# An unused strip of 96 bytes at the top of SBUF, in a kernel with two MLP layers behind a spectral layer

## The chip, the cores and the metric

The kernel runs on one core of a Trainium2 chip. The metric is the device time of one execution in microseconds (us); the times before are given as the median of three runs. All arithmetic is in float32, or in the float32 form that TensorE takes in one pass (fp32r), with each operand split into a high and a low part where one pass would lose too much.

## What is computed

The reference chains three parts over 2 x 3008 tokens of width 256:

```python
X = np.fft.rfft(x, axis=1)                      # along the 3008 positions
Yr = Xr @ w_r - Xi @ w_i + b_r
Yi = Xr @ w_i + Xi @ w_r + b_i
Yr, Yi = soft_threshold(Yr, 0.01), soft_threshold(Yi, 0.01)
x = np.fft.irfft(Yr + 1j * Yi, n=3008, axis=1).reshape(6016, 256)

h = x @ w_in            # 256 -> 2048
x = (h * sigmoid(1.702 * h)) @ w_out            # 2048 -> 256
h = x @ w_in2
out = (h * sigmoid(h)) @ w_out2
```

## The kernel before

The two Fourier transforms are matmuls with folded cosine and sine matrices (line 341 forward, line 344 back), the frequency-wise product with w_r and w_i is line 469, and the thresholds are lines 486 and 487. The result lies in one big tile, yt, of 128 partitions x 2 x 6016 floats; both MLP layers read it and write back into it in place.

The MLP takes its tokens in blocks of 1024 (five of them, and one of 896), each cut into two halves of 512 (448) columns. `group(l, i, p, hook)` handles layer l, block i and one pair p of hidden chunks of 128: there are 2 x 6 x 8 = 96 such pairs. In each it makes seven products of the input weights (line 736, by a Strassen-like scheme), each of three matmuls (high by high, high by low, low by high): 21 matmuls. The activation is line 739, its high part line 741, its low part line 746. The products with the output weights are `out_mm` (line 708): 24 matmuls for each pair. So a pair is 45 matmuls, and each has a moving operand of 512 or 448 columns and its own weight load of 128 x 128.

The moving operands of line 736 are tiles named x, those of line 708 tiles named g. Both, and the tiles of the earlier stages that have the same life (xt, f, fl, fd), are slots of 2048 bytes of the pool "xt": 14 slots of class x0 and 12 of class x1. The pool is opened on the right side of SBUF, whose pools are laid from the top of the memory downwards in the order in which they are opened: "xt" first, then, in turns, "lv0", "wc", "mid" and "yt". What is opened later on that side lies below. The pools of the left side (m, the weights, cv, raw and others) are laid from the bottom upwards and are not touched by what happens on the right side. The stationary operands of the MLP, wi and wo, are on the left side; those of the inverse transform are fh on the left and fl in slots of "xt", with slices of m (left side) as moving operands.

The scheduler places instructions with a timing of its own where the code does not fix their order; nearly all of the MLP is under a fixed order (`region('rest0')` and the like).

Of the kernel before, what the change touches and what calls it, by code (L numbers as in the profile page):

```python
# [9 lines left out]
F32 = mybir.dt.float32  # L10
# [11 lines left out]
P = 128  # L22
# [34 lines left out]
def spectral_mlp_kernel(ctx, tc, xin, mfwd, minv, wc, bias, w_in1, w_out1, w_in2, w_out2, outT):  # L57
# [11 lines left out]
    def region(name):  # L69
        m = CFG.get(name, "none")  # L70
        if "man" in ex:
            ex.pop("man").close()
        ex["man"] = ExitStack()
        if m != "none":
            ex["man"].enter_context(tc.manual_schedule(engines=None if m == "all" else {getattr(mybir.EngineType, e) for e in m.split(",")}))


    def opened(name, side=None, bufs=1, **kw):
        ex[name] = ExitStack()
        return ex[name].enter_context(tc.tile_pool(name=name, bufs=bufs, side=side, reuse_waits="tile", **kw))  # L80

    def closed(*names):
        for name in names:
            ex.pop(name).close()
# [2 lines left out]
    wia_p = opened("wia", "left", NPR // 2)  # L87
    cv_p = opened("cv", "left", 2)
    dram_p = opened("dram", bufs=1, space=bass.MemoryType.DRAM)
    xt_p = opened("xt", "right", 12)  # L90
    ps_p = [opened(f"ps{i}", bufs=4, space=PS) for i in range(2)]

# [235 lines left out]
    xt = {}  # L328
# [220 lines left out]
    yt = yt_p.tile([P, 2, NT], F32, name="yt")  # L549
# [330 lines left out]
    while pend:  # L880
        out_next()
    region('end')
    closed("ps1", "ps0", "wib", "yt", "xt", "cv", "wia", "m", "dram")

# [143 lines left out]
```

## Time and profile before

| | |
|---|---|
| median of three runs | 1226.17 us (1226.07 to 1228.11) |
| the profiled execution | 1227.75 us, span of its instructions 1225.6 us |
| mean granted TensorE clock | 0.998 |
| TensorE busy | 1193.8 us (97%) |
| ScalarE busy | 751.5 us (61%) |
| VectorE busy | 670.7 us (55%) |
| GpSimd busy | 526.9 us (43%) |

TensorE's row counts a matmul from its start to a modelled end, and matmuls overlap, so the duration of one is longer than its share of the time. The distance between two starts is what one costs; the chain of work that ended last and the listing in order of time show starts. Weight loads (PEld) run beside matmuls.

### The profile page before, as it was taken

The page shows a single profiled execution, that of the slowest core. Times are in us where ns is not written, and L with a number is a line of the kernel's source. Part 1 is how long each engine was busy: PE and PEld are TensorE (multiplying, and loading weights), DVE is VectorE, ACT ScalarE, POOL GpSimd, SP SyncE. Part 2 cuts the span into 40 slices and gives each one's busy share as a digit, 9 for nine tenths or more (in the row PEclk, how much of TensorE's full clock was granted, in tenths as well). Part 3 has the DMA queues.
Part 4 walks back from the last instruction along what each step waited for, and adds up shares of the span by engine and source line. Part 5 has one row for each costly group of instructions (what it writes and reads, how often), then busy time and mean ns, then how long its engine had stood idle before and what let it go on. Part 6 is the DMA issues. An engine that isn't in the chain of part 4 may idle for free.

```text
span 1225.6 us, 14433 instructions
## 1 busy us (share of the span) xinstructions
PE 1193.8 (97%) x5044; PEld 934.9 (76%) x5044; DVE 670.7 (55%) x1001; ACT 751.5 (61%) x1422; POOL 526.9 (43%) x429
## 2 busy tenths in 40 slices
PE   7999988799999999999999999999999999999998
PEld 4744488577787887877888978878888888888897
DVE  6868999777447556366464463352442533523422
ACT  1433443577667667667667776675665766755665
POOL 2543334463444444444445755433333333333332
PEclk9999999999999999999999999999999999999999
DMA  7642121121011110110120100000000000000000
GB/s 255 195 150 87 43 101 60 28 67 35 26 44 35 40 38 26 52 43 26 35 60 9 53 26 26 1 35 1 1 35 1 1 35 1 35 1 1 35 1 30
DMA packets 27274, 54.44 MB, mean 44 GB/s; under 512 B 2369, under 2 KB 11585, under 8 KB 26434
## 3 DMA queue, kind: packets, MB, share of 16 engines
q1 hardware_dynamic: 26018, 45.03, 11.1%
q0 software_dynamic: 1184, 8.50, 1.9%
q8 instruction: 39, 0.64, 0.2%
q14 instruction: 33, 0.27, 0.1%
HBM read 41.85 MB, written 11.67 MB: 44 GB/s over the span
## 4 chain that ended last, share of the span: by engine, by line
PE 68%; DVE 15%; ACT 7%; issue 4%; DMA 4%; POOL 1%; SPq 0%; DVEq 0%; ACTq 0%; POOLq 0%
PE o L708 35%; PE x L736 32%; ACT yt L739 2%; ACT g L741 2%; DMA raw<-in_wo 1%; DMA raw<-in_wi 1%; PE psf L341 1%; DVE fl L99 1%; DVE yt L628 1%; DVE f L501 1%; DVE cv_a L169 1%; DVE cv_c L167 1%; DVE th L487 1%; DMA raw<-in_x 1%; DVE cv_c L168 1%
## 5 line engine op out<-in xcount | busy, mean ns | idle before, releaser
L746 POOL TENSOR_TENSOR g<-yt,g 128x512 fp32r<-128x512 f32 (+1 forms) x282 | 368.1, 1318 | 533.3 <-DVE g L746 278.6
L708 PE MATMUL o<-g,wo 128*128 128x512 f32 (+1 forms) x2304 | 574.2, 391 | 4.6 <-POOL wo L99 4.6
L736 PE MATMUL x<-x,wi 128*128 128x512 f32 (+1 forms) x2016 | 513.3, 393 | 10.5 <-DVE yt L757 4.2
L708 PEld LDWEIGHTS o<-g,wo 128*128 128x128 f32 x2304 | 432.1, 188 | 100.8 <-POOL wo L99 6.3
L736 PEld LDWEIGHTS x<-x,wi 128*128 128x128 f32 x2016 | 376.7, 188 | 103.3 <-DVE yt L778 5.3
L739 ACT ACTIVATE yt<-yt 128x512 f32<-128x512 f32 (+1 forms) x288 | 179.1, 622 | 283.0 <-DVE yt L778 232.7
L741 ACT CAST g<-yt 128x512 fp32r<-128x512 f32 (+1 forms) x384 | 234.1, 611 | 11.8
L778 DVE TENSOR_TENSOR yt<-yt,x 128x512 f32<-128x512 f32 (+1 forms) x96 | 64.8, 675 | 230.3 <-PE x L736 230.2
L757 DVE TENSOR_TENSOR yt<-yt,x 128x512 f32<-128x512 f32 (+1 forms) x96 | 64.9, 676 | 163.5 <-ACT yt L755 159.3
L746 DVE TENSOR_TENSOR g<-yt,g 128x512 fp32r<-128x512 f32 (+1 forms) x102 | 71.1, 697 | 75.0 <-ACT g L741 73.8
L469 PE MATMUL psm<-wc_s,xt 128*128 128x512 f32 x192 | 84.5, 592 | 0.0
L469 PEld LDWEIGHTS psm<-wc_s,xt 128*128 128x128 f32 x192 | 36.4, 190 | 43.4 <-issue 41.2
L341 PE MATMUL psf<-m,xf 128*128 128x376 f32 (+2 forms) x208 | 61.4, 458 | 7.3 <-DVE xf L300 6.2
L659 DVE TENSOR_TENSOR x<-yt,x 128x512 fp32r<-128x512 f32 (+1 forms) x48 | 46.5, 970 | 34.6 <-ACT x L656 34.6
L781 DVE TENSOR_TENSOR yt<-yt,x 128x512 f32<-128x512 f32 (+1 forms) x96 | 64.8, 675 | 0.6
L341 PEld LDWEIGHTS psf<-m,xf 128*128 128x128 f32 x208 | 39.4, 200 | 28.7 <-DVE xf L300 7.3
L739 ACT ACTIVATE yt<-x 128x512 f32<-128x512 f32 (+1 forms) x96 | 56.2, 585 | 2.2 <-PE x L736 2.2
L772 ACT COPY yt<-x 128x512 f32<-128x512 f32 (+1 forms) x96 | 55.7, 581 | 0.8 <-PE x L736 0.8
L755 ACT COPY yt<-x 128x512 f32<-128x512 f32 (+1 forms) x96 | 54.9, 571 | 2.1 <-PE x L736 2.1
L770 ACT COPY yt<-x 128x512 f32<-128x512 f32 (+1 forms) x96 | 54.9, 572 | 0.0
L344 PE MATMUL psi<-m,fh 128*128 128x376 f32 (+3 forms) x208 | 48.0, 319 | 3.6 <-DVE rt L607 2.8
L224 POOL TENSOR_TENSOR cv_a<-cv_a,cv_c 128x512 f32<-128x512 f32 x26 | 37.9, 1457 | 14.6 <-DVE cv_c L171 10.6
(90 smaller groups left out, 798.3 us busy)
## 6 DMA issues: line engine op xcount, KB each, us to landing
raw<-in_wi SPq DMA_DIRECT2D x32, 256.0 KB, 3.1
raw<-in_wo SPq DMA_DIRECT2D x16, 512.0 KB, 3.6
raw<-in_x SPq DMA_DIRECT2D x12, 512.0 KB, 5.1
out_t<-yt SPq DMA_DIRECT2D x20, 256.0 KB, 2.0
m<-in_mi POOLq DMA_DIRECT2D x4, 1128.0 KB, 6.0
w_out<-cv_a SPq DMA_DIRECT2D x13, 256.0 KB, 2.0
cv_ld<-w_out SPq DMA_DIRECT2D x13, 256.0 KB, 2.6
m<-in_mi POOLq DMA_DIRECT2D x2, 1134.0 KB, 6.0
```

Of the source, the lines that this page charges most:

```text
L341: nc.tensor.matmul(ps, hi[:, c : c + P], m[:, k, :w], start=i == 0, stop=i == last)
L469: nc.tensor.matmul(t, x[xi][:, mm], wc_s[:, mm, off : off + 2 * D], start=(n == 0), stop=(n == 3 and grp == 1))
L708: nc.tensor.matmul(acc[h, mm], st, mv, start=first and k == 0, stop=last and k == 2)
L736: nc.tensor.matmul(ps, st, mv, start=first and m == 0, stop=m == 2, skip_group_check=True)
L739: nc.scalar.activation(g, g if src is None else src, func)
L741: nc.scalar.copy(gh, g)
L746: eng.tensor_sub(gl, g, r32(gh))
L755: nc.scalar.copy(y1, X)
L757: nc.vector.tensor_add(y1, y1, Y)
L772: nc.scalar.copy(y3, X)
L778: nc.vector.tensor_add(y2, y2, X)
L781: nc.vector.tensor_add(y3, y3, Z)
```

## The change

One more pool, "gap", is opened on the right side ahead of "xt", with one tile of 128 partitions x 24 floats. Nothing reads or writes it. It takes the 96 bytes below the top, so that "xt" and all that is opened on that side after it begin 96 bytes lower. The pool is closed where the others are.

```diff
     dram_p = opened("dram", bufs=1, space=bass.MemoryType.DRAM)
+    opened("gap", "right").tile([P, 24], F32, name="gap")
     xt_p = opened("xt", "right", 12)
     ps_p = [opened(f"ps{i}", bufs=4, space=PS) for i in range(2)]
...
-    closed("ps1", "ps0", "wib", "yt", "xt", "cv", "wia", "m", "dram")
+    closed("ps1", "ps0", "wib", "yt", "xt", "gap", "cv", "wia", "m", "dram")
```

## Rows read from the trace of the kernel before

**Rows 1.** The page: busy us (share) xinstructions; chain that ended last, by line.
```profile
PE 1193.8 (97%) x5044; PEld 934.9 (76%) x5044; DVE 670.7 (55%) x1001; ACT 751.5 (61%) x1422; POOL 526.9 (43%) x429
...
PE o L708 35%; PE x L736 32%; ACT yt L739 2%; ACT g L741 2%; DMA raw<-in_wo 1%; DMA raw<-in_wi 1%; PE psf L341 1%; DVE fl L99 1%; DVE yt L628 1%; DVE f L501 1%; DVE cv_a L169 1%; DVE cv_c L167 1%; DVE th L487 1%; DMA raw<-in_x 1%; DVE cv_c L168 1%
```

**Rows 2.** Busy us by stretch (x instructions), granted clock (PEclk), DMA share, GB/s.
```profile
222.00:1222.00 1000.00, 990.19 (x4296) 803.47 (x4295) 487.34 (x697) 669.67 (x1213) 437.68 (x336) 1.00 0.08 26
1222.00:1225.60 3.60, 0.00 (x0) 0.00 (x0) 0.00 (x0) 0.32 (x1) 0.00 (x0) 0.96 0.56 205
```

**Rows 3.** Matmuls by shape: xcount | busy us, mean ns of one | idle before.
```profile
L708 PE MATMUL o<-g,wo 128*128 128x512 f32 x1920 | 487.9, 395 | 4.6 <-POOL wo L99 4.6
L736 PE MATMUL x<-x,wi 128*128 128x512 f32 x1680 | 435.6, 397 | 8.8 <-DVE yt L757 4.2 <-ACT yt L772 1.6 <-ACT rt L585 1.3
L708 PE MATMUL o<-g,wo 128*128 128x448 f32 x384 | 86.3, 367 | 0.0
L469 PE MATMUL psm<-wc_s,xt 128*128 128x512 f32 x192 | 84.5, 592 | 0.0
L736 PE MATMUL x<-x,wi 128*128 128x448 f32 x336 | 78.9, 370 | 1.7 <-DVE x L659 0.9 <-ACT yt L772 0.4
```

**Rows 4.** Pieces of the chain that ended last: start us, us, what.
```profile
665.63 2.46 PE o L708 x12
...
674.87 2.46 PE o L708 x12
...
840.92 2.80 PE o L708 x12
...
851.42 2.80 PE o L708 x12
```

**Rows 5.** The same operations by shape on ScalarE, GpSimd and VectorE, as rows 3.
```profile
L741 ACT CAST g<-yt 128x512 fp32r<-128x512 f32 x320 | 198.0, 620 | 9.8
L98 ACT CAST wo<-cv_ld 128x512 fp32r<-128x512 f32 x13 | 8.1, 624 | 0.0
L746 POOL TENSOR_TENSOR g<-yt,g 128x512 fp32r<-128x512 f32 x234 | 312.1, 1347 | 467.8 <-DVE g L746 273.8 <-PE x L736 77.7 <-DVE yt L712 41.3
L99 POOL TENSOR_TENSOR wi<-cv_s,wi 128x512 fp32r<-128x512 f32 x8 | 10.8, 1346 | 0.9 <-PE o L708 0.9
L778 DVE TENSOR_TENSOR yt<-yt,x 128x512 f32<-128x512 f32 x80 | 54.9, 686 | 187.0 <-PE x L736 186.9
L481 DVE TENSOR_TENSOR sd<-us,psm 128x512 f32<-128x512 f32 x12 | 8.1, 678 | 0.0
```

**Rows 6.** Inverse transform, 376 columns, TensorE in order of time: start us, us, what.
```profile
200.66 0.50 PE L344 MATMUL psi<-m,fh 128*128 128x376 f32 x2
...
201.17 0.51 PE L344 MATMUL psi<-m,fh 128*128 128x376 f32 x2
...
201.69 0.51 PE L344 MATMUL psi<-m,fh 128*128 128x376 f32 x2
...
202.21 0.50 PE L344 MATMUL psi<-m,fh 128*128 128x376 f32 x2
```

**Rows 7.** Inverse transform, 378 columns, TensorE in order of time, as rows 6.
```profile
156.85 0.51 PE L344 MATMUL psi<-m,fh 128*128 128x378 f32 x2
...
157.37 0.50 PE L344 MATMUL psi<-m,fh 128*128 128x378 f32 x2
157.71 0.34 PE L344 MATMUL psi<-m,fl 128*128 128x378 f32 x1
157.89 0.51 PE L344 MATMUL psi<-m,fh 128*128 128x378 f32 x2
158.24 0.34 PE L344 MATMUL psi<-m,fl 128*128 128x378 f32 x1
158.41 0.51 PE L344 MATMUL psi<-m,fh 128*128 128x378 f32 x2
```

**Rows 8.** The page's DMA issues: KB each, median us from issue to landing.
```profile
out_t<-yt SPq DMA_DIRECT2D x20, 256.0 KB, 2.0
```

## The prediction

> **What bounds the kernel now.** I read the page's first part, then the chain of work that ended last, then the busy time by stage. TensorE is busy for 1193.8 us of a span of 1225.6 us, and its two lines of the MLP, 708 and 736, carry 35% and 32% of the chain [rows 1]. From 222 us to 1222 us TensorE is busy for 990.19 of 1000 us, at a granted clock of 1.00 (the 2.4 GHz level), while VectorE has 487, ScalarE 670 and GpSimd 438 us of work in the same stretch [rows 2]. So in four fifths of the span nothing but the distance from one matmul to the next sets the time. A faster or slower vector operation would vanish in the slack there.
>
> That distance is not the mean duration of 395 ns that the listing by shape gives [rows 3], because matmuls overlap. It is read from the chain. One pair of hidden chunks is 45 matmuls (1920 + 1680 + 384 + 336 over 96 pairs [rows 3]). Where all of them have 512 columns, the same piece of the chain comes back after 851.42 - 840.92 = 10.50 us, and with 448 columns after 674.87 - 665.63 = 9.24 us [rows 4]. That is 233.3 ns and 205.3 ns for each matmul. At 2.4 GHz the columns alone would take 213.3 and 186.7 ns, so each matmul costs 20.0 and 18.7 ns more than its columns. 3600 matmuls have 512 columns and 720 have 448: 840 us + 147.8 us = 987.8 us of the span.
>
> **The change part by part.** It allocates 96 bytes that nothing reads or writes. The built program has the same instructions in the same order on every engine, with the same waits; only addresses differ. By the program's addresses, which no row shows, every slot of x and g and the big tile yt begins 96 bytes past a multiple of 128 before, and on a multiple of 128 after. Weights (wi, wo), m, raw and PSUM stay; wi and wo are on multiples of 128 already. The tiles of the middle stage (us, sd, th, wc_s) go the other way, from 64 past to 96 past. Since no instruction, wait or transfer is added, the whole question is whether an operation's time depends on where its operand begins. I take the engines one by one.
>
> ScalarE, VectorE, GpSimd: the trace has the same operation on slots of both kinds. The 512-element cast takes 620 ns from yt to g (both 96 past) and 624 ns between tiles on a multiple of 128. GpSimd's subtraction takes 1347 ns on yt and g and 1346 ns on tiles on a multiple of 128. VectorE's addition with a PSUM operand takes 686 ns on yt (96 past) and 678 ns on sd (64 past) [rows 5]. The largest difference is 8 ns in 686, on an engine with half of its time free; I cost all three at nothing. If that cover were gone, the 288 additions of lines 757, 778 and 781 (96 each) would be worth 288 x 8 ns = 2.3 us.
>
> TensorE, the term that decides: 4320 matmuls whose moving operand is an x or a g slot. Every such slot has the same place modulo 2048, so the MLP has no case to compare. The inverse transform has one. There the moving operand is a slice of m, and slices of 376 floats (1504 bytes) begin 0, 32, 64 or 96 bytes past a multiple of 128; slices of 378 floats also begin at odd multiples of 8. The matmuls run back to back in nines, one triple for each row block j.
>
> In the nine with 376 columns the first triple begins its slices at 0, 32, 0 and takes 201.17 - 200.66 = 0.51 us. The third triple begins them at 64, 96, 64 and takes 202.21 - 201.69 = 0.52 us [rows 6]. In pieces of 128 bytes the first touches 36 and the third 39. A piece is 32 columns, or 13.3 ns at 2.4 GHz, so a read limited by such pieces would make the third 40 ns longer. It is 10 ns longer, which is the resolution of the rows.
>
> In the nine with 378 columns the second triple begins at 104, 32, 104 and touches 75 pieces of 64 bytes; it takes 157.89 - 157.37 = 0.52 us. The third begins at 80, 8, 80, touches 72, and also takes 158.41 - 157.89 = 0.52 us [rows 7]. Three pieces of 16 columns would be 20 ns. Its pairs even go the other way: 0.34 us with 50 pieces, 0.35 us with 48.
>
> The nines as a whole take 1.55 and 1.56 us, that is 172.2 and 173.3 ns for a matmul against 156.7 and 157.5 ns of columns: 9.9% and 10.1% above the columns, at mixed places [rows 6, 7]. The MLP's, all at 96 past, are 9.4% (512) and 10.0% (448) above theirs [rows 4]. If beginning at 96 past cost much, the MLP would stand out; it doesn't. I take 0 ns per matmul.
>
> The rest: 192 matmul instructions of the middle stage get wc_s at 96 past instead of 64 [rows 3]; at most one 64-byte piece more each is 192 x 6.7 ns = 1.3 us, at least nothing, and I take nothing, by rows 7. The 24 stores of yt land after 2.0 us and only the last one stands at the end, within the 3.6 us behind the last matmul [rows 2, 8]; a tenth of its landing would be 0.2 us.
>
> Sum: 4320 x 0 + 0 + 0 = 0. The profiled execution took 1227.75 us with a span of 1225.6 us, so it is 1227.75 us again; it lies 1.6 us (0.13%) above the median of the runs shown, 1226.17 us. For the median I predict 1226.2 us.
>
> **The rivals.** The first: the moving operand is read in pieces that the address cuts. In pieces of 64 bytes, 512 floats from 96 past touch 33 and from 0 past 32; 448 floats 29 and 28. One piece less is 6.7 ns x 4320 = 28.8 us: 1197.4 us. In pieces of 128 bytes it is 13.3 ns, 57.6 us: 1168.6 us. For it: the matmul's excess over its columns grows with the columns (15.5 ns at 376, 20.0 ns at 512), as if reading were the limit, and a limit is where a cut costs. Against it: rows 6 and 7. [...] A partial effect, a fixed piece of start-up that shrinks by 0.6 to 2.3 ns, would give 2.5 to 10 us: 1216 to 1223.7 us.
>
> The furthest form of it is that the whole excess over the columns is the address: 3600 x 20.0 + 720 x 18.7 ns = 85.4 us, 1140.8 us. It would need the nines at 0 past to run at their columns' time, and the triple that begins at 0, 32, 0 has 0.51 us against 0.47. [...]
>
> The rival on the other side: while one matmul streams, the weights of the next are loaded, and after the change both operands lie on the same place modulo 128. If two reads on the same place hinder each other, every matmul of the MLP pays. In the nines three of nine matmuls have both operands on the same place; their mean excess is at most 0.5 points of 156.7 ns above that of the 512-column matmuls (9.9% against 9.4%), 0.8 ns, which is 2.4 ns for each of the three. 4320 x 2.4 ns = 10.4 us: 1236.5 us. It makes the kernel slower from 0.57 ns a matmul on (2.45 us / 4320). For it: operands never share their place in the MLP before. Against it: the excess of 448 columns, 10.0% without any shared place, is as high as that of the nines.
>
> That the strip doesn't move the slots is no rival; the addresses show that it does.
>
> **How the numbers follow.** Within 0.2% (2.45 us, about what a measurement of this kernel can tell from no change) is the forecast: 0.55, with its own range of 1223.7 to 1228.6 us. Faster: 0.05 for a partial effect, 0.13 for pieces of 64 bytes, 0.05 for 128 bytes, 0.04 for the whole excess; together 0.27. Slower: 0.12 for shared places up to 1236.5 us, 0.06 for more than that; together 0.18. Neither side alone brings the forecast to 8 in 10, so the range takes in the partial gain, the 64-byte pieces and the shared places: 1197 to 1236.5 us, leaving out 0.15.
>
> **What would show it.** Right: the piece of the chain in the MLP still comes back after 10.50 us (512 columns) and 9.24 us (448), and the stages ahead of 222 us keep their length. Pieces of 64 bytes: 10.20 us (45 x 226.7 ns). Pieces of 128 bytes: 9.90 us. Shared places: up to 10.61 us. The forecast is wrong as soon as that period moves by more than 0.03 us, since 96 pairs make 2.9 us of it. If the period is much shorter, the next limit to look at is ScalarE, which has 670 us of work in the 1000 us stretch [rows 2], and then waits of lines 757 and 778 would appear on TensorE.

## The result, and the profile after

The changed kernel takes 1208.21 us (median of 4 runs, 1206.23 to 1210.07), the kernel before on the same chip 1226.12 us (1225.52 to 1228.11). The ratio is 0.9848 with an interval of 0.9836 to 0.9859: 1.5% faster, where no change was forecast. The profiled execution took 1207.06 us with a span of 1204.9 us, 20.7 us under the span of before; the medians differ by 17.9 us. Of the 20.7 us, 18.7 lie in the MLP and 2.0 ahead of it: its first matmul starts at 207.91 us instead of 209.93. The 2.0 us are no gain of the change: over the eleven profiles of the whole kernel that moment lies between 207.9 and 210.6 us, whatever the addresses. All lines of the changed kernel from 90 on are one higher, so line 709 after is line 708 before.

The page after, busy time and the chain of work that ended last by line; compare with [rows 1]:

```profile
PE 1172.0 (97%) x5044; PEld 936.6 (78%) x5044; DVE 669.5 (56%) x1001; ACT 751.8 (62%) x1422; POOL 524.5 (44%) x429
...
PE o L709 33%; PE x L737 30%; PE psm L470 7%; PE psf L342 4%; ACT yt L740 3%; PE psi L345 2%; ACT g L742 2%; DVE yt L758 1%; DMA raw<-in_x 1%; DVE yt L779 1%; ACT yt L756 1%; DVE x L660 1%; DVE yt L629 1%; ACT x L657 1%; DVE cv_a L170 1%
```

TensorE has 21.8 us less busy time for the same 5044 matmuls, while the other engines moved by at most 2.4 us. The two lines of the MLP lost two points each of the chain, and the additions of lines 758 and 779 are now among the lines that it lists.

The chain after, start us, us, what, in the blocks with 448 columns and in those with 512; compare with [rows 4]:

```profile
648.35 2.44 PE o L709 x12
...
657.47 2.44 PE o L709 x12
...
666.59 2.44 PE o L709 x12
...
880.67 2.72 PE o L709 x12
...
890.87 2.72 PE o L709 x12
...
901.07 2.72 PE o L709 x12
```

The piece of 45 matmuls comes back after 10.20 us instead of 10.50 (512 columns), and after 9.12 us instead of 9.24 (448). That is 226.7 ns instead of 233.3 for a matmul, and 202.7 instead of 205.3. The gain is there: a matmul of the MLP that waits for no other engine follows the one before it 6.7 or 2.7 ns sooner. 3600 x 6.67 ns + 720 x 2.67 ns make 24.0 + 1.9 = 25.9 us, more than the 18 us that the medians show. Where the rest went is told in the part on why the prediction was wrong.

The groups by shape after, which answer to [rows 3] and [rows 5] (xcount | busy, mean ns | idle before it, releaser):

```profile
L709 PE MATMUL o<-g,wo 128*128 128x512 f32 x1920 | 476.7, 390 | 4.0 <-POOL wo L100 4.0
L737 PE MATMUL x<-x,wi 128*128 128x512 f32 x1680 | 428.3, 393 | 10.2 <-DVE yt L758 4.2 <-DVE yt L779 2.7 <-ACT yt L773 2.0
...
L470 PE MATMUL psm<-wc_s,xt 128*128 128x512 f32 x192 | 84.5, 592 | 0.0
...
L742 ACT CAST g<-yt 128x512 fp32r<-128x512 f32 x320 | 198.1, 621 | 9.8
```

The mean duration of an MLP matmul of 512 columns fell by 5 and 4 ns. The middle stage (line 470, 84.5 us and 592 ns before too) and the cast (620 ns before) are as they were.

### The profile page after: what moved, and what is told of

It is laid out like the page before. It is cut to its first block, busy times and chain, and to the rows that moved or that the text cites. A ratio compares the mean times of both kernels' runs of the same rounds, so it can differ in the third digit from the quotient of the medians.

```text
span 1204.9 us, 14433 instructions
## 1 busy us (share of the span) xinstructions
PE 1172.0 (97%) x5044; PEld 936.6 (78%) x5044; DVE 669.5 (56%) x1001; ACT 751.8 (62%) x1422; POOL 524.5 (44%) x429
## 4 chain that ended last, share of the span: by engine, by line
PE 76%; DVE 10%; ACT 8%; issue 4%; DMA 1%; POOL 0%; SPq 0%; DVEq 0%; ACTq 0%; POOLq 0%
PE o L709 33%; PE x L737 30%; PE psm L470 7%; PE psf L342 4%; ACT yt L740 3%; PE psi L345 2%; ACT g L742 2%; DVE yt L758 1%; DMA raw<-in_x 1%; DVE yt L779 1%; ACT yt L756 1%; DVE x L660 1%; DVE yt L629 1%; ACT x L657 1%; DVE cv_a L170 1%
## 5 line engine op out<-in xcount | busy, mean ns | idle before, releaser
L709 PE MATMUL o<-g,wo 128*128 128x512 f32 (+1 forms) x2304 | 562.1, 386 | 4.0 <-POOL wo L100 4.0
L737 PE MATMUL x<-x,wi 128*128 128x512 f32 (+1 forms) x2016 | 505.3, 389 | 12.1 <-DVE yt L758 4.2
L742 ACT CAST g<-yt 128x512 fp32r<-128x512 f32 (+1 forms) x384 | 234.2, 612 | 11.8
L470 PE MATMUL psm<-wc_s,xt 128*128 128x512 f32 x192 | 84.5, 592 | 0.0
```

Source lines behind the costliest of these rows:

```text
L470: nc.tensor.matmul(t, x[xi][:, mm], wc_s[:, mm, off : off + 2 * D], start=(n == 0), stop=(n == 3 and grp == 1))
L709: nc.tensor.matmul(acc[h, mm], st, mv, start=first and k == 0, stop=last and k == 2)
L737: nc.tensor.matmul(ps, st, mv, start=first and m == 0, stop=m == 2, skip_group_check=True)
L742: nc.scalar.copy(gh, g)
```

## The experiments

In what follows **distance** is the first byte of a matmul's moving operand less the first byte of its weights, modulo 512, by the addresses of the built program. In the MLP before it is 352 for both kinds of matmul (96 modulo 256); after, 256 (0 modulo 256). The theories: **A**, the place of the moving operand alone counts, in pieces of 64 bytes that the address cuts (with pieces of 128 bytes it is called **B**); **C**, the distance between the two operands counts.

**table.** A kernel that does the matmuls alone, one group behind the other (68 groups, run once), with the moving operand and the weights at chosen places:

```
for n, at, wat in CASES:
    o = ps_p.tile([P, 512], F32, tag="ps", name=f"n{n}c{at}m{wat}w")
    for i in range(48):
        w = wat // 4 + P * (i % 4)
        nc.tensor.matmul(o[:, :n], wt[:, w : w + P], mv[:, at // 4 : at // 4 + n], start=True, stop=True)
```

> The kernel leaves out the whole computation and writes zeros: it only runs 69 groups of 48 matmuls back to back, each group with its own number of columns, its own first byte of the moving operand (counted modulo 128 from a tile that begins on a multiple of 128) and its own first byte of the weights. The distance of two starts is read for each group. Theory A (the moving operand is read in pieces of 64 bytes): 512 columns take 226.7 ns where the moving operand begins on a multiple of 64 bytes (0, 64, 128, 192) and 233.3 ns at every other place, whatever the weights' place. Theory B (pieces of 128 bytes): 226.7 ns at 0 and 128 only, 233.3 ns at 64. Theory C (what counts is whether moving operand and weights begin at the same place modulo 128): 226.7 ns where the two places are equal (0 and 0, 32 and 32, 64 and 64, 96 and 96), 233.3 ns elsewhere. With 448 columns A expects 202.7 ns at 0 and 64 and 205.3 ns at 32 and 96; with 376 and 378 columns A expects differences only where the number of pieces differs.

Its timeline on TensorE: start us, us from the first start to the last end, what. The name has the columns behind n, the place of the moving operand behind c, that of the weights behind m:

```profile
112.13 11.36 PE L104 MATMUL n512c64m0w<-mv,wt 128*128 128x512 f32 x48
...
224.17 11.05 PE L104 MATMUL n512c32m32w<-mv,wt 128*128 128x512 f32 x48
...
279.66 11.07 PE L104 MATMUL n512c64m64w<-mv,wt 128*128 128x512 f32 x48
```

47 distances in time from start to start and one matmul's duration of 0.39 us make a group, so 11.36 us is 233.4 ns a matmul and 11.05 to 11.07 us is 227 ns. The moving operand stands at 64 in the first and in the third row; what differs is where the weights are. With equal places (0, 32, 64 or 96) every group settled at 226.6 to 226.7 ns; of the unequal ones of 512 columns the lowest was 228.9 (96 against 32), and the others took 231 to 240. That is against A and B and for C.

**strip32, strip64.** The strip with 32 and with 64 bytes:

```diff
-    opened("gap", "right").tile([P, 24], F32, name="gap")
+    opened("gap", "right").tile([P, 8], F32, name="gap")
```

(strip64: `[P, 16]`.) x and g then begin 64 and 32 bytes past a multiple of 128; their distances are 320 and 288.

> The strip has 32 bytes instead of 96, so x, g and yt begin 64 past a multiple of 128. Theory A (pieces of 64 bytes): as the changed kernel, 10.20 us for a pair of chunks with 512 columns, ratio to the kernel before 0.985 (0.980 to 0.990). Theory B (pieces of 128 bytes) and theory C (same place as the weights, which are on multiples of 128): as the kernel before, 10.50 us, ratio 1.000 (0.997 to 1.003).

> The strip has 64 bytes, so x, g and yt begin 32 past a multiple of 128. All of theory A, B and C: as the kernel before, 10.50 us for a pair, ratio 1.000 (0.997 to 1.003). If any move of these slots helps, by where they stand against other tiles and not by a multiple of 64, it would be near 0.985.

strip64 took 1226.29 us, ratio 0.9997 [0.9988, 1.0007]: no change. strip32 took 1211.95 us (1211.27 to 1224.06 in 6 runs), ratio 0.9894 [0.9863, 0.9926]: seven tenths of the gain by the ratios. By themselves these two would have fitted pieces of 64 bytes: a place that is a multiple of 64 gains, one that isn't doesn't; and strip32 goes against C as it was first put, that only equal places gain. The next two kernels break the pieces.

**left96.** The strip not above x and g but below the weights, so that x and g stay 96 bytes past a multiple of 128 and the weights move up to it:

```diff
+    opened("low", "left").tile([P, 24], F32, name="low")
...
-    opened("gap", "right").tile([P, 24], F32, name="gap")
...
```

> No strip at the top; instead an unused strip of 96 bytes at the bottom, which moves the tiles of the other side (weights, m, fh, raw, cv) up by 96 bytes, so that weights begin 96 past a multiple of 128 as x and g do. Theory A and theory B: x and g have not moved, so 10.50 us for a pair and a ratio of 1.000 (0.997 to 1.003), unless weight loads are cut as well, which would show as a longer pair. Theory C: both operands are on the same place, 10.20 us, ratio 0.985.

1209.37 us, ratio 0.986 [0.9845, 0.9874], as good as the change. The chain of left96 in a block of 512 columns has the same period, 893.65 - 883.45 = 10.20 us:

```profile
883.45 2.72 PE o L709 x12
...
893.65 2.49 PE o L709 x11
```

So it isn't where x and g begin. A and B are out, and so are pieces of any other size.

**table2.** The matmuls alone again, run once, in groups of 60 that each start on an idle TensorE, over all distances in steps of 32 bytes:

> The kernel leaves out the whole computation and writes zeros. It runs groups of 60 matmuls, each group from a fresh start (it waits until ScalarE has read the group before), for the distance between the first byte of the moving operand and that of the weights, in steps of 32 bytes over 512. The first table, left96 and strip32 have felled the pieces of 64 and 128 bytes (theories A and B) and leave theory C: what counts is the distance of the two operands. Two forms of it. C128 (the distance modulo 128): 512 columns take 226.7 ns at distances 0, 128, 256 and 384 and 233 ns elsewhere. C256 (modulo 256; the first table had 232.5 ns at 128): 226.7 ns at 0 and 256 and 232 to 235 ns elsewhere, with weights at 0 and at 128 alike. If only the very same place counts (modulo 512 or more), 226.7 ns at 0 alone; but the changed kernel has 256 and 226.7 ns. With 448 columns no theory has a number; the kernels gave 205.3 ns at 352 and 202.7 ns at 256.

Some of its groups in the timeline on TensorE. With 512 columns a group is a longer first distance of about 0.34 us, 58 further ones and one matmul's duration of 0.39 us (0.31 and 0.37 us with 448 columns), so 13.88 us is 226.7 ns a matmul:

```profile
56.05 14.01 PE L105 MATMUL n512c64m0w<-mv,wt 128*128 128x512 f32 x60 [0.73 <-ACT ev L106]
...
85.78 14.26 PE L105 MATMUL n512c128m0w<-mv,wt 128*128 128x512 f32 x60 [0.73 <-ACT ev L106]
100.78 14.32 PE L105 MATMUL n512c160m0w<-mv,wt 128*128 128x512 f32 x60 [0.73 <-ACT ev L106]
...
145.81 13.88 PE L105 MATMUL n512c256m0w<-mv,wt 128*128 128x512 f32 x60 [0.73 <-ACT ev L106]
...
190.16 14.27 PE L105 MATMUL n512c352m0w<-mv,wt 128*128 128x512 f32 x60 [0.73 <-ACT ev L106]
...
295.18 13.90 PE L105 MATMUL n512c128m128w<-mv,wt 128*128 128x512 f32 x60 [0.73 <-ACT ev L106]
...
515.17 12.28 PE L105 MATMUL n448c320m0w<-mv,wt 128*128 128x448 f32 x60 [0.68 <-ACT ev L106]
528.14 12.59 PE L105 MATMUL n448c352m0w<-mv,wt 128*128 128x448 f32 x60 [0.68 <-ACT ev L106]
```

All values, in ns from one start to the next, once a group has settled (from about its twelfth matmul on):

| distance mod 256 | 0 | 32 | 64 | 96 | 128 | 160 | 192 | 224 |
|---|---|---|---|---|---|---|---|---|
| 512 columns | 226.7 | 233.3 | 229.0 | 233.2 | 233.4 | 234.4 | 233.3 | 233.3 |
| 448 columns, below 256 | 202.7 | 200.0 | 200.0 | 205.3 | 204.2 | 200.0 | 202.3 | 204.4 |

With 512 columns the second 256 bytes repeat the first (groups of 60 at distances that are 256 apart differ by at most 0.02 us of 14); with 448 they do too, but for 206.7 at 256 against 202.7 at 0. Weights at 128 with the moving operand at 128 or at 384 give 226.7 again; with it at 0 or 256, 233.2 and 232.4. So the distance modulo 256 counts, and the MLP's two values are both here: 233.2 at 96 (before), 226.7 at 0 (after). 448 columns behave differently: the change brings them 2.7 ns, and 320, with 200.0 ns, is better than both of the MLP's distances. Slices of 376 and 378 columns vary little at the distances of this table, 170.1 to 173.4 ns.

**strip224, both96.** A strip of 224 bytes puts x and g on a multiple of 128, as the change does, but at the distance 128. Both strips of 96 bytes at once leave x and g on a multiple of 128 as after the change and put the weights 96 bytes past one as in left96, at the distance 160:

```diff
-    opened("gap", "right").tile([P, 24], F32, name="gap")
+    opened("gap", "right").tile([P, 56], F32, name="gap")
```

```diff
+    opened("low", "left").tile([P, 24], F32, name="low")
...
```

> The strip has 224 bytes, 128 more than in the changed kernel: x, g and yt again begin on multiples of 128, and the distance from moving operand to weights is 128 modulo 256, where it was 0 in the changed kernel. Theories A and B (64 or 128 bytes of the moving operand alone) and C128 (distance modulo 128): as the changed kernel, 10.20 us for a pair of chunks with 512 columns, ratio 0.985. C256 (distance modulo 256): near the kernel before, 10.46 us by the first table's 232.5 ns at 128, ratio 0.995 to 1.000.

> Both strips of 96 bytes, at the top and at the bottom: x and g begin on multiples of 128 as in the changed kernel, weights 96 past one; the distance is 160 modulo 256. Each strip alone gave a ratio near 0.985. Theories A and B: as the changed kernel, 10.20 us, 0.985. C128 and C256: the two moves take the gain from each other; by the first table's 234.2 ns at 160 a pair takes 10.54 us, ratio 1.000 to 1.004.

strip224 took 1223.91 us, 0.9973 [0.9964, 0.9983]; both96 took 1227.64 us, 1.0008 [0.9998, 1.0018]. The chains of strip224 and then of both96 in a block of 512 columns:

```profile
880.48 2.80 PE o L709 x12
...
890.98 2.10 PE o L709 x9
```

```profile
881.25 2.81 PE o L710 x12
...
891.79 2.34 PE o L710 x10
```

The periods are 10.50 us (233.3 ns; the table has 233.4 at 128) and 10.54 us (234.2 ns; the table has 234.4 at 160). Alignment to 128 bytes thus brings at most the 0.27% of strip224 by itself, and two shifts that each bring 1.4 to 1.5% bring nothing together.

**x_only, g_only.** The slots of x and of g in two pools, with strips that give one of the two kinds of matmul the distance 256 and leave the other at a poor one (352 and 224):

```diff
-    xt_p = opened("xt", "right", 12)
+    xg_p = opened("xg", "right", 12)
+    opened("gapb", "right").tile([P, 24], F32, name="gapb")
+    xt_p = opened("xt", "right", 14)
+    opened("gapc", "right").tile([P, 8], F32, name="gapc")
...
-        return xt_p.tile([P, 2 * D], dtype, tag=f"x{cls}", name=name, bufs=14 if cls == 0 else 12)
+        return (xg_p if cls else xt_p).tile([P, 2 * D], dtype, tag=f"x{cls}", name=name, bufs=14 if cls == 0 else 12)
...
```

(g_only has a strip of 24 floats above xg and one of 8 between the pools, and none below.)

> The slots of x move down by 96 bytes, those of g and the tile yt stay at 96 past a multiple of 128 (two strips among two pools; the instructions and their order are those of the kernel before). If the cost belongs to each matmul by its own operands, the 21 matmuls of line 736 in a pair take 226.7 ns and the 24 of line 708 233.3 ns: 10.36 us, and 1680 x 6.7 + 336 x 2.7 ns = 12.1 us at most, of which the changed kernel kept seven tenths: ratio 0.990 to 0.994. If the alternation of the two kinds upsets the gain, 10.50 us and 1.000.

> The slots of g move down by 96 bytes (distance 256 to the weights), those of x by 128 (distance 224), yt by 128. Moving x alone to 256 gave a ratio of 0.998, a tenth of the whole, because a matmul reaches 226.7 ns only some seven matmuls after the distance has changed, and the two kinds alternate by 6 to 12. The same is expected for g, whose runs are of 6 and 12: 10.40 to 10.47 us for a pair, ratio 0.993 to 0.999. If instead line 708 alone had made the gain, 0.987.

x_only took 1225.15 us, 0.9984 [0.9975, 0.9994]; g_only 1220.3 us, 0.9941 [0.9924, 0.9957]. The savings are 0.16% and 0.59%, together half of the change's 1.52%: they don't add up. The chains of x_only and then of g_only in a block of 512 columns show why:

```profile
889.96 2.80 PE o L711 x12
892.76 1.39 PE x L739 x6
894.15 1.41 PE o L711 x6
895.55 2.08 PE x L739 x9
```

```profile
889.18 2.75 PE o L711 x12
...
899.58 2.52 PE o L711 x11
```

In x_only the matmuls of line 739 have the good distance, but in runs of 6 or 9 between others that don't; they take 231.7 and 231.1 ns, not 226.7. In g_only it is line 711 that has it, in runs of 6 and 12: its run of 12 takes 229 ns a matmul, and the period is 10.40 us. Read from the starts of single matmuls, the runs of 12 of g_only stay at 226 to 227 ns from their sixth matmul on, while the runs of 9 of x_only still go up and down between 224 and 236 ns. Here a good distance paid in full only where it lasted.

**table3.** Whose weights: those that a matmul uses, or the next one's, loaded while it streams (in the kernel before a load of line 708 begins at 840.53 us, and the matmuls of line 736 ahead of it run until 840.93)? Moving operands and weights alternate between the places 0 and 96, so that either the own weights are at the distance 96 and the next ones at 0 (`own`), or the other way (`next`); beside these, distances in steps of 4 bytes.

> The kernel leaves out the whole computation and writes zeros; groups of 60 matmuls of 512 columns from a fresh start. The second table has shown that the distance of the two operands modulo 256 sets the time of a matmul; open is which weights count. While a matmul streams, the weights of the next one are loaded. In the groups named apart..own each matmul stands at a distance of 32, 64, 96 or 128 bytes to its own weights and at 0 to those of the next; in the groups named apart..next it is the other way round. If the next weights count (two reads at the same time meet), the own groups take 226.7 ns and the next groups 229 to 235 ns, those with 96 and 128 about 233 ns. If a matmul's own weights count, the reverse. The rest steps the distance by 4 bytes from 0 to 64 and around 256: if 34 steps of 16 cycles at 2.4 GHz are the least, nothing is under 226.7 ns; if places between have less waiting, some group is.

```profile
85.88 14.07 PE L106 MATMUL apart96ownq<-mv,wt 128*128 128x512 f32 x60 [0.73 <-ACT ev L107]
100.68 14.31 PE L106 MATMUL apart96nextq<-mv,wt 128*128 128x512 f32 x60 [0.73 <-ACT ev L107]
...
160.32 14.46 PE L106 MATMUL n512c4q<-mv,wt 128*128 128x512 f32 x60 [0.73 <-ACT ev L107]
...
444.07 14.65 PE L106 MATMUL n512c244q<-mv,wt 128*128 128x512 f32 x60 [0.73 <-ACT ev L107]
```

With the other weights 96 bytes off, equal places for the next weights give 229.9 ns, for the own weights 234.1; at 32 bytes it is 230.0 and 231.7, at 64 both give 231.7, and at 128 it is 230.0 and 236.7. The next weights seem to weigh more, but neither alone reaches 226.7; and as the places alternate, the next weights stand where the previous ones stood, so these two can't be told apart here. This doesn't settle it. In steps of 4 bytes the time jumps: 226.7 at 0, 28, 60, 252 and 256; 236.6 at 4; 240.0 at 244; nothing lies under 226.7. A distance nearer to a multiple of 256 isn't steadily better.

**best, again.** The change with the 448-column slices of x and g begun 64 bytes into their slots (distance 320), and the change itself once more on the same chip:

```diff
+    def cut_of(t, n):
+        return t[:, :n] if n == 512 else t[:, 16 : 16 + n]
...
-            gh = slot(1, F32R, "g")[:, :n]
+            gh = cut_of(slot(1, F32R, "g"), n)
...
```

(The low part of g and both parts of x are cut in the same way.)

> The changed kernel, and in the blocks of 448 columns x and g begin 64 bytes into their slots, so that their distance is 320 instead of 256. By the second table 448 columns take 200.0 ns at 320 (202.7 ns were measured in the changed kernel): a pair of these blocks takes 9.00 us instead of 9.12 us. 720 x 2.7 ns = 1.9 us at most, some of it given back to waits: ratio to the kernel before 0.982 to 0.985, 1 to 2 us under the changed kernel beside it.

> The changed kernel once more, beside the version above on the same chip: ratio to the kernel before 0.984 to 0.986.

best took 1206.63 us (1205.82 to 1207.18), 0.9832 [0.9817, 0.9846] of the kernel before; the change, again, 1208.66 us (1208.1 to 1209.9), 0.985 [0.9836, 0.9865]. The chain of best in the blocks of 448 columns:

```profile
648.46 2.40 PE o L712 x12
...
657.46 2.40 PE o L712 x12
```

9.00 us, 200.0 ns a matmul, as the second table has it. 720 x 2.67 ns = 1.9 us was to be had over the change, and the medians differ by 2.0 us; the ranges of the runs don't overlap. In the profiles the two blocks with 448 columns are shorter by 1.4 us together, so a part of the 2.0 us may be chance. It is the fastest version of the study.

**One distance, two values.** With 512 columns seven kernels (the one before among them) have the table's value within 0.5 ns in their blocks of layer 1. The profiled run of strip32 is the exception; its chain, and the busy times of a stretch with the granted clock (columns as in rows 2):

```profile
881.02 2.80 PE o L709 x12
...
891.52 2.80 PE o L709 x12
```

```profile
870.00:960.00 90.00, 90.00 (x388) 73.08 (x387) 35.10 (x49) 57.28 (x102) 32.52 (x25) 0.95 0.03 12
```

It has 10.50 us, 233.3 ns, where the second table has 229.0 at 64. That run took 1224.06 us, the other five 1211.27 to 1212.74, and its granted clock was 0.95 through the MLP, where every other profile has 1.00. But the first table has 233.4 ns for a moving operand at 64 and weights at 0 at a clock of 1.00, and 228.9 for 96 against 32, the same distance; and a run of strip64 with a mean clock of 0.947 took 1227.31 us, within the range of its other nine. So the clock isn't needed for the longer value: at this distance the same stream is found with one or the other.

The same holds for 448 columns. At the distance 256 the change has 202.7 ns, the second table 206.7, and left96 has both in one run: 202.7 in layer 0 and 206.7 in all but the first pair of its block in layer 1. At 0 the first table has 206.7 and the second 202.7, at 32 they have 206.7 and 200.0, and strip64 has 206.7 (12 in 2.48 us) where the table has 200.0 at 288; before, strip32, strip224, both96 and best agree within 0.4 ns. What decides between two values isn't shown. At the two distances on which the change rests, 0 and 96 with 512 columns, no stream in which the distance lasts has a second value: 226.6 to 226.7 and 233.2 to 233.3 ns.

## Why the prediction was wrong

**The bound: right for layer 1, too wide for layer 0.** The distance from one matmul to the next set the time where the gain came. But rows 1 give lines 708 and 736 67% of the chain, while the stretch for which the prediction says that nothing else sets the time is four fifths of the span. The chain of the kernel before by line, first for the MLP's layer 0, then for layer 1:

```profile
by line: PE o L708 35.3%; PE x L736 33.6%; issue 5.9%; ACT yt L739 4.9%; ACT g L741 2.6%; DVE yt L757 1.9%; DVE cv_a L169 1.6%; DVE yt L778 1.5%; ACT yt L755 1.3%; DVE cv_c L167 1.2%; DVE cv_c L168 1.2%; ACT x L656 1.1%; DVE cv_c L170 0.9%;
```

```profile
by line: PE o L708 50.3%; PE x L736 43.8%; issue 1.1%; ACT yt L739 1.1%; ACT g L741 1.1%; DVE x L659 0.6%; DVE yt L712 0.4%; ACT yt L772 0.3%; ACT yt L770 0.2%; DVE yt L778 0.2%; ACT yt L755 0.2%; ACT x L656 0.2%; ACT yt L712 0.2%; DVE g L7
```

TensorE's busy time of 990 in 1000 us hid this, since the matmuls overlap (395 ns the mean one, 233.3 ns from start to start): one that starts late need not leave a gap.

**No new instruction, ScalarE, VectorE and GpSimd at nothing: right.** The cast takes 621 ns after against 620, VectorE's addition of line 779 685 against 686, GpSimd's subtraction of line 747 1342 against 1347, in the groups by shape.

**The middle stage at nothing: right**, 84.5 us before and after.

**"I take 0 ns per matmul": this step failed.** It is 6.67 ns for 3600 matmuls and 2.67 ns for 720. The step asked the inverse transform [rows 6, 7] whether a matmul's time depends on where its moving operand begins, found no dependence, and left it at that. That the moving operand's place alone doesn't decide was right, as left96 shows with x and g unmoved; the question was too narrow. What counts is the place of the moving operand relative to the weights, and the inverse transform couldn't show it, because its nines mix places: by the program's addresses no distance lasts for more than two matmuls, and x_only shows that even runs of 6 and 9 matmuls at one distance collect only a part. Slices of 376 columns also depend little on the distance, by 3.3 ns at most in table2. Slices of 378 columns do depend on it where it lasts, as the first table has them at 8 and at 80 bytes, 169 and 177 ns a matmul:

```profile
559.48 8.27 PE L104 MATMUL n378c8m0w<-mv,wt 128*128 128x378 f32 x48
...
584.16 8.64 PE L104 MATMUL n378c80m0w<-mv,wt 128*128 128x378 f32 x48
```

The triple of rows 7 at 80, 8 and 80 took 0.52 us like the one before it, so the prediction read as no effect what mixing may have hidden. The argument beside it, that the MLP would stand out if 96 past were a bad place, compared it with those mixed nines: an average, not a best case.

**The rival of 64-byte pieces: right size, wrong mechanism.** It named 6.7 ns, a period of 10.20 us and 1197.4 us, and the period of 512 columns came out at exactly that. But it gives 6.7 ns for 448 columns too, where 2.7 came, and it falls with left96 and strip224. The period with 512 columns alone would have made it look proven.

**The rival of shared places: right quantity, wrong sign.** It alone spoke of the relation of both operands, and it priced them as hindering each other on the same place. Matmuls of 512 columns have their shortest spacing, 226.7 ns, with both on the same place, counted modulo 256 and not 128: at a distance of 128 they take 232.4 to 233.4 ns. The 2.4 ns at most that it read out of the nines was again a value of mixed places.

**"If the period is much shorter, the next limit to look at is ScalarE": right as to waits on other engines, wrong as to a limit.** ScalarE is busy for 62% of the span after, so it isn't the limit; but waits for it and for VectorE where one block gives way to the next took back a part. Of 25.9 us, 18.7 us were kept in the MLP. From the first matmul of x in a block to that of the next block, the six blocks of layer 1 went from 503.3 to 491.2 us, 12.1 of the 12.95 us that half of the sum makes; those of layer 0 from 508.5 to 501.9 us, 6.6 of 12.95. So nearly all of the loss is in layer 0, and a third of that in its first block, where lines 708 and 736 hold a fifth of the chain. That block before and then after (columns as in rows 2):

```profile
209.93:300.84 90.91, 81.29 (x330) 62.09 (x331) 70.89 (x110) 62.21 (x113) 46.23 (x34) 0.98 0.15 44
```

```profile
207.91:298.60 90.69, 81.42 (x332) 63.83 (x332) 70.92 (x110) 62.17 (x113) 46.18 (x34) 0.94 0.14 44
```

It is shorter by 0.22 us instead of 2.40. The granted clock was lower there after, but left96, with 0.98 as before, took 90.71 us, so the clock isn't the reason. A later block of each layer, layer 0 first; the kernel before:

```profile
472.18:557.05 84.87, 84.55 (x362) 67.42 (x361) 48.94 (x65) 56.92 (x102) 38.44 (x28) 1.00 0.11 38
...
889.06:973.06 84.00, 84.00 (x361) 67.58 (x360) 33.00 (x46) 54.71 (x98) 31.30 (x24) 1.00 0.04 13
```

and the kernel after:

```profile
467.07:550.45 83.38, 82.55 (x362) 67.25 (x361) 48.80 (x65) 57.00 (x102) 38.29 (x28) 1.00 0.11 39
876.42:958.02 81.60, 81.60 (x361) 67.57 (x360) 32.79 (x46) 54.73 (x98) 31.22 (x24) 1.00 0.04 14
```

The block of layer 1 keeps TensorE busy throughout and is shorter by the full 2.40 us (8 pieces x 0.30 us). The block of layer 0 is shorter by 1.49 us: TensorE stood still for 0.32 us before and for 0.83 us after, and the other 0.40 us are lost in matmuls that start late without a gap between them. The timeline on TensorE near the end of that block of layer 0, where the x of the next block are made ready, before:

```profile
545.26 2.38 PE L736 MATMUL x<-x,wi 128*128 128x512 f32 x9
...
553.45 1.66 PE L736 MATMUL x<-x,wi 128*128 128x512 f32 x6 [0.21 <-ACT yt L772]
```

and after (idle before it and what ended that, in brackets):

```profile
538.70 2.33 PE L737 MATMUL x<-x,wi 128*128 128x512 f32 x9 [0.46 <-DVE yt L779]
...
546.89 1.66 PE L737 MATMUL x<-x,wi 128*128 128x512 f32 x6 [0.37 <-ACT yt L773]
```

There, matmuls of line 737 wait for an addition on VectorE (line 779) and a copy on ScalarE (line 773), whose work takes as long as before (685 and 590 ns; 686 and 590 before); a TensorE that came sooner waited there for 0.46 us where it had not waited, and for 0.37 us instead of 0.21. The prediction's guess that the waits would be those of lines 757 and 778 (758 and 779 after) names one of the two that show here, 779; the other is line 773 on ScalarE.

**The time** lies inside the range of 1197 to 1236.5 us, on the side that had a chance of 0.27. That is luck: the range reached so far down for the partial effect (1216 us and more) and for the 64-byte pieces (1197.4 us), and the cause was neither.

**What stays open.** Why the distance modulo 256 counts, no run shows. Which weights count, the matmul's own or the next one's, table3 left undecided. And why a distance can have two values, 64 with 512 columns and several with 448, no run tells.

## What to carry to other kernels

Where a stream of matmuls is bound by its own spacing and takes longer than its columns, look at the addresses: the distance between the moving operand and the weights, not the alignment of either, was worth 3% of a matmul's time here (fp32r, 512 columns, new weights for each matmul), and it should be the same good one for all kinds of matmul that alternate (one kind alone saved 0.16% or 0.59%, both together 1.52%). A short kernel that repeats the matmul at many distances shows in one run what a search through allocations would find by chance; as one run can show one of two values, the kernel itself has the last word. And evidence that something has no effect holds only for what varied in it: here the place varied and the relation never lasted.

## What the runs showed of the hardware

Single matmuls of 512 columns, with new weights for each, took 226.7 to 240.0 ns at a granted clock of 1.00, by the distance of their operands. In the second table the shortest spacings of 512, 448 and 376 columns are 226.7, 200.0 and 170.1 ns, 0.417 ns for each column from 448 to 512 and 0.415 from 376 to 448. By an estimate from these, 512 columns alone are 213 ns, as the prediction has them at its 2.4 GHz (0.417 ns a column), and no distance came nearer to that than 6%. The groups of the first table are matmuls alone, with no work for VectorE, ScalarE or GpSimd among them; the time of a matmul still depends on where its own two operands lie to each other.

A matmul of float32 operands in the middle stage stands in the trace as two records: 192 for the 96 of line 469, busy for 84.5 us, which is 0.88 us for each. One of fp32r operands in the MLP stands as one.

The spacings come back to a tenth of a nanosecond in kernels that have little in common: 200.0, 202.7, 205.3, 226.7 and 233.3 ns. Some distances have two of them: 64 with 512 columns has 229.0 and 233.3, 256 with 448 columns 202.7 and 206.7. And 226.7 ns needs no equal places: distances of 28 and 252 bytes give it as well as 0.
